# Attention and a token mixer on one core: the first four heads' exponentials and v stay four bytes wide

## The chip, the cores and the metric

One core of one Trainium2 chip runs the whole program. TensorE (PE, with its weight loads PEld), VectorE (DVE), ScalarE (ACT) and GpSimd (POOL) each work through a queue of their own in order; SyncE (SP) issues the transfers. The metric is the device time of one execution in microseconds; three runs of the kernel before stand here.

## The reference, cut to what matters

```python
scores = scale * np.matmul(q, k.transpose(0, 1, 3, 2))      # 8 batches, 8 heads, 576 positions, 64 wide
scores = np.where(block_i >= block_j, scores, -1e9)         # blocks of 64 positions
attn = np.exp(scores - np.max(scores, axis=-1, keepdims=True))
attn = attn / (np.sum(attn, axis=-1, keepdims=True) + 1e-09)
x = np.matmul(attn, v)                                      # heads side by side: 512 channels
theta = x @ w_theta
zr, zi = x * np.cos(theta), x * np.sin(theta)
u = x + w_tok_r @ zr + w_tok_i @ zi                         # over the 576 positions of a batch
out = u + np.maximum(u @ w_ch, 0.0)
```

All inputs and the output are four-byte or wider. The kernel keeps that accuracy mostly by splitting a number into a high and a low two-byte part and making three products: high by high, high by low, low by high.

## The kernel before

A batch is four pairs of heads, 64 heads in all. For a pair, `scores_wide`, `scores_narrow` and `scores_first` make the scores on PE, batches 0 to 2 straight from the four-byte q and k (the constant `WHOLE`), later ones from parts. Per head, DVE takes maxima (`maxima`, L632), ACT the exponentials into the four-byte tile `t` (L645). The exponentials must then be turned, keys to the partitions. For the first eight heads (`PE_TURNED`) PE does it: `turn_up` (L670) transposes blocks of 128 columns into the PSUM banks from which the scores came, `turned_high` copies them as two-byte high parts into the tile `pt` (a copy on ACT or DVE, L430 and L432), `turned_low` subtracts on DVE and writes the low parts (L435). A head has three such pieces at most: A (8 blocks, 1024 columns), B (4 blocks, 512), and for the even head of a pair "4" (1 block). Later heads are split before the turning (`high`, `low`) and turned by transfers. `weighted` (L704) then makes the head's 15 blocks by v, three products a block, with v's high part from `v_first` (L422, L424, L426) and low part from `v_second` (L572, DVE); `normalise` (L716 to L722) divides.

When all heads of a batch are done, the mixer runs: `theta` on PE (L840, L843), the angle's rest and size, sines on ACT (L881, L883), products with x (`times_x`, L892), z's high and low parts (L430, L435), `mix` on PE (L916), u and its parts, `channel` on PE (L939) and the output. The three weight matrices arrive at the start as eight-byte numbers, are cut on ACT, POOL and DVE (L470 to L506), scaled and split.

Nothing is scheduled by itself: `emit` walks the table `ORDER`, a list of step numbers, and so writes each engine's queue; `BANKS` gives each PSUM use its bank and `PLACES` a letter (A, D, P) for each step that may run on more than one engine. The tables cover the whole program, all eight batches.

Of the kernel before, what the change touches and what calls it, by code (L numbers as in the profile page):

```python
# [212 lines left out]
]  # L213
BANKS = (
    "6036634613301236460123451012346501235400123650123100123640123640123540123460123560123560123560123450123540123540"
    "1235401234601235401234601234601234501235401235601235601234601235601236501234601236401236501236524650165044562445"
    "1366654015041066656146605041531566625545056616403655450046560146652046315014405544561042543015410645564641503045"
    "126452542562535304460316014405260435142"
)
# [1011 lines left out]
```

## Time and profile before

| what | us |
|---|---|
| median of 3 runs | 658.3 (657.48 to 658.71) |
| the profiled execution | 657.96 |
| its span, first to last instruction | 656.2 |
| PE busy | 620.3 |
| DVE busy | 578.4 |
| ACT busy | 511.3 |
| POOL busy | 352.3 |

The span is the time between the first and the last instruction; 1.8 us lie around it. Busy time is the time in which at least one instruction of the engine was under way; as matmuls overlap their neighbours, a busy PE need not be at its peak.

### The profile page before, as it was taken

Reading aid. Unit: us, or ns where it says so; the run is one execution under the profiler, and the core shown is the slowest. Engines: PE = TensorE matmul, PEld = TensorE weight load, DVE = VectorE, ACT = ScalarE, POOL = GpSimd, SP = SyncE. Lnnn points to the kernel's source line nnn. Section 1 sums busy time; section 2 is a strip of 40 time slices with the busy share of each in tenths; the row PEclk is TensorE's granted clock in tenths of the full one; section 3 lists DMA queues with packets and bytes.
Section 4 is the critical chain, followed back from the end, with each engine's and each line's share of the span. In section 5 each row is a group of like instructions: output and inputs, shape, how many; then the busy total and the mean of one; then the engine's idle time right before and its main releaser. Section 6 shows DMA issues by size and latency. Waiting matters only on the chain. (4 is left out here: it accounts for less than half of the span.)

```text
span 656.2 us, 18226 instructions
## 1 busy us (share of the span) xinstructions
PE 620.3 (95%) x7474; PEld 459.1 (70%) x7474; DVE 578.4 (88%) x1153; ACT 511.3 (78%) x803; POOL 352.3 (54%) x392
## 2 busy tenths in 40 slices
PE   5689979999999999999999999999999999899997
PEld 3377657775887677767778667875776677757775
DVE  4999999898999898998999999998999988766655
ACT  5999899777975999979988889998998987026212
POOL 4335574553565456545684248654684586553520
PEclk9799996999999999999999999999999999999999
DMA  9965697989698579968997887999898666920101
GB/s 350 394 210 151 110 198 167 209 156 219 141 241 163 116 154 240 204 122 192 214 223 160 147 236 169 181 177 191 178 212 157 114 104 142 179 42 1 56 19 72
DMA packets 242403, 110.03 MB, mean 168 GB/s; under 512 B 229904, under 2 KB 229904, under 8 KB 242320
## 3 DMA queue, kind: packets, MB, share of 16 engines
q1 hardware_dynamic: 242320, 108.88, 76.1%
q8 instruction: 58, 0.95, 0.6%
q14 instruction: 25, 0.20, 0.1%
HBM read 42.01 MB, written 9.44 MB: 78 GB/s over the span
## 5 line engine op out<-in xcount | busy, mean ns | idle before, releaser
L916 PEld LDWEIGHTS <-zh 128*128 128x128 f16 x1152 | 112.7, 98 | 31.5 <-issue 1.7
L916 PE MATMUL g<-wT_h,zh 128*128 128x288 f16 x396 | 113.4, 286 | 2.0 <-DVE xT L955 2.0
L916 PE MATMUL g<-wT_l,zh 128*128 128x288 f16 x396 | 113.2, 286 | 0.0
L916 PE MATMUL g<-wT_h,zl 128*128 128x288 f16 x396 | 113.2, 286 | 0.0
L704 PE MATMUL g<-v,pt 128*128 128x65 f16 x2880 | 100.9, 195 | 7.0 <-DVE xn L722 5.4
L704 PEld LDWEIGHTS <-pt 128*128 128x128 f16 x2880 | 97.4, 98 | 13.3 <-issue 4.5
L632 DVE TENSOR_REDUCE m<-s 128x1 f32<-128x576 f32 (+3 forms) x132 | 85.1, 672 | 2.7 <-PE s L595 2.2
L435 DVE TENSOR_TENSOR p<-t,p 128x1600 f16<-128x1600 f32 (+4 forms) x47 | 78.3, 1668 | 3.1 <-ACT p L430 2.5
L430 ACT CAST p<-t 128x1536 f16<-128x1536 f32 (+4 forms) x51 | 68.0, 1337 | 2.7 <-DMA pt<-p 2.0
L435 POOL TENSOR_TENSOR p<-t,p 128x1536 f16<-128x1536 f32 (+4 forms) x17 | 45.0, 2650 | 46.5 <-ACT p L430 32.0
L916 PEld LDWEIGHTS <-zl 128*128 128x128 f16 x576 | 56.4, 98 | 18.6 <-DVE zl L435 2.1
L645 ACT ACTIVATE t<-s,m,size 128x576 f32<-128x576 f32 (+1 forms) x80 | 59.8, 780 | 7.2 <-POOL m L640 5.2
L840 PEld LDWEIGHTS <-xT 128*128 128x128 f16 x384 | 35.7, 98 | 39.4 <-issue 3.7
L632 DVE TENSOR_REDUCE m<-g 128x1 f32<-128x192 f32 (+2 forms) x156 | 54.1, 370 | 7.6 <-PE g L595 7.5
L939 PEld LDWEIGHTS <-wch_h 128*128 128x128 f16 x512 | 47.8, 98 | 15.8 <-issue 3.3
L435 POOL TENSOR_TENSOR zl<-aa,zh 128x512 f16<-128x512 f32 (+1 forms) x34 | 42.5, 1256 | 27.0 <-ACT zh L430 25.7
L645 ACT ACTIVATE t<-g,m,size 128x320 f32<-128x320 f32 (+2 forms) x100 | 49.4, 535 | 9.7 <-POOL m L640 9.1
L916 PE MATMUL s<-wT_h,zl 128*128 128x288 f16 x180 | 51.5, 286 | 1.8 <-DVE zl L435 1.8
L916 PE MATMUL s<-wT_h,zh 128*128 128x288 f16 x180 | 51.5, 286 | 0.0
L916 PE MATMUL s<-wT_l,zh 128*128 128x288 f16 x180 | 51.5, 286 | 0.0
L892 POOL TENSOR_TENSOR aa<-aa,xn 128x256 f32<-128x256 f32 (+1 forms) x58 | 43.6, 761 | 9.7 <-ACT aa L883 8.5
L939 PE MATMUL g<-uh,wch_h 128*128 128x288 f16 x160 | 45.8, 286 | 1.8 <-ACT t L645 1.2
(199 smaller groups left out, 1668.9 us busy)
## 6 DMA issues: line engine op xcount, KB each, us to landing
rv<-in_v SPq DMA_DIRECT2D x16, 768.0 KB, 5.8
rq<-in_q SPq DMA_DIRECT2D x16, 640.0 KB, 5.6
rk<-in_k SPq DMA_DIRECT2D x16, 576.0 KB, 4.7
out<-xT SPq DMA_DIRECT2D x32, 288.0 KB, 3.6
w_raw<-in_w_tok SPq DMA_DIRECT2D x5, 576.0 KB, 5.8
pt<-in_w_tok SPq DMA_DIRECT2D x4, 576.0 KB, 8.6
w_raw<-in_w_theta SPq DMA_DIRECT2D x4, 512.0 KB, 7.6
w_raw<-in_w_ch SPq DMA_DIRECT2D x4, 512.0 KB, 5.1
```

What stands on the lines that cost most here:

```text
L430: nc.scalar.copy(out=out, in_=x)
L435: engine_of(on).tensor_tensor(out=out, in0=x, in1=y, op=ALU.subtract)
L632: nc.vector.tensor_reduce(out=self.m[:, i:i + 1], in_=self.scores_of(i), axis=AX.X, op=ALU.max)
L645: nc.scalar.activation(out=t_parts[self.hh][:, to:to + n], in_=self.scores_of(i), func=AF.Exp, scale=self.scales()[0], bias=self.m[:, NI + ...
L704: nc.tensor.matmul(o[:, i, :], lhsT=source[:, block, :], rhs=vv[:, slot, hh, :], start=first, stop=last)
L840: nc.tensor.matmul(g, lhsT=xT[:, xx + i, :], rhs=ww[:, dt, :], start=first, stop=last)
L892: engine_of(on).tensor_tensor(out=cd, in0=cd, in1=self.xns[dt][:, i0:i0 + ni, :], op=ALU.mult)
L916: nc.tensor.matmul(g, lhsT=zz[:, kk, cols], rhs=ww[:, kk, ts], start=(n == 0 and kk == k0 and nn == 0), stop=n == 4 and kk == k0 + ni - 1 ...
L939: nc.tensor.matmul(g[:, 0:HS], lhsT=ww[:, dt, e * P:(e + 1) * P], rhs=uu[:, dt, th * HS:(th + 1) * HS], start=dt == 0 and n == 0, stop=dt ...
```

## The change

For heads 0 to 3 the turned exponentials are copied out of PSUM as four-byte numbers, into the room that the two parts had, and v is scaled into a four-byte tile. `turned_low` and `v_second` fall away for them, and `weighted` makes one four-byte product a block. The four-byte v tiles share their room with the q and k parts of batch 3 and later, which become slices of two fixed tiles. `ORDER`, `BANKS` and `PLACES` are new throughout: of the 903 letters 274 differ, of the 375 banks 84; `ORDER` has 3444 steps for 3456.

```diff
+WIDE_HEADS = 4
...
 PLACES = (
-    "ADPPAPPAAPDPPDAPAAPAPDDPPAAPAPPAADAADAPPAAPAAPAAPAAAPADPAPAPAPPAAPAPADAAPAAPAPAPAPPAAPAPAPAADPDPAPPAPPADAPPPPPPP"
...
+    "PDPDAPDDPPDPPDPPAAPAPPAAAAAPAADAPDAAPAPPAAAAAPAAPAADPADPAPAPDPDAAPDPADADPADDAPAPAPPAAPAPAPAAPDDPAPPAPPAPPPAPDAPP"
...
+    room = {"qh": (0, S + D), "kh": (S + D, S), "ql": (2 * S + D, S + D), "kl": (3 * S + 2 * D, S)}
+    qk_room = [const.tile([P, 4 * S + 2 * D], F16, name=f"qk{i}") for i in range(QK_BUFS)]
+    v_wide = [x[:, 0:4 * NV * (D + 1)].bitcast(F32).rearrange("p (a h d) -> p a h d", a=NV, h=2) for x in qk_room]
+    for part in v_wide:
+        nc.gpsimd.memset(part[:, :, :, D:D + 1], 1.0)
+        nc.gpsimd.memset(part[64:P, 0, :, D:D + 1], 0.0)
+        nc.gpsimd.memset(part[0:64, NV - 1, :, D:D + 1], 0.0)
...
         def part(self, tag):
-            return ld.tile([P, S + D if tag[0] == "q" else S], F16, tag=tag, name=tag, bufs=QK_BUFS)
+            at_, n = room[tag]
+            return qk_room[self.p % QK_BUFS][:, at_:at_ + n]
...
         def v_first(self, on):
-            scaled(on, self.v1[:, :, :, 0:D], self.raw("v"), self.mixer.scales["v"].up)
+            to = v_wide[self.p % 2] if 2 * self.p < WIDE_HEADS else self.v1
+            scaled(on, to[:, :, :, 0:D], self.raw("v"), self.mixer.scales["v"].up)
...
+    def wide_of(turned):
+
+        return turned.rearrange("p a c -> p (a c)").bitcast(F32).rearrange("p (a c) -> p a c", c=P)
...
+            if self.n < WIDE_HEADS:
+                at_ = {"A": 4, "B": 0, "4": 12}[piece]
+                return x, wide_of(self.turned)[:, at_:at_ + n, :], None
...
+                if self.n < WIDE_HEADS:
+                    for j, (at_, slot) in enumerate(blocks):
+                        nc.tensor.matmul(o[:, i, :], lhsT=wide_of(source)[:, at_, :], rhs=v_wide[pair.p % 2][:, slot, hh, :],
+                                         start=j == 0, stop=j == len(blocks) - 1)
+                    continue
...
-        add(("v2", p), pair.v_second, [("v1", p)])
+        if 2 * p >= WIDE_HEADS:
+            add(("v2", p), pair.v_second, [("v1", p)])
...
-                        add(("th", n, x), step_of(h.turned_high, x), [("tp", n, x)] + w_free, on="AD")
-                        add(("tl", n, x), step_of(h.turned_low, x), [("th", n, x)],
-                            leaves={"A": [("s1", p, hh, k) for k in range(2)], "B": [("s2", p, hh)], "4": [("t4", n)]}[x])
+                        leaves = {"A": [("s1", p, hh, k) for k in range(2)], "B": [("s2", p, hh)], "4": [("t4", n)]}[x]
+                        add(("th", n, x), step_of(h.turned_high, x), [("tp", n, x)] + w_free, leaves=leaves if n < WIDE_HEADS else (), on="AD")
+                        if n >= WIDE_HEADS:
+                            add(("tl", n, x), step_of(h.turned_low, x), [("th", n, x)], leaves=leaves)
```

## Rows read from the trace of the kernel before

**Rows 1.** The page's head and table of engines: busy us (share), instructions.

```profile
span 656.2 us, 18226 instructions
PE 620.3 (95%) x7474; PEld 459.1 (70%) x7474; DVE 578.4 (88%) x1153; ACT 511.3 (78%) x803; POOL 352.3 (54%) x392
```

**Rows 2.** Stretches: us, busy time (instructions) by engine, PE clock, DMA share, GB/s.

```profile
13.30:23.50 10.20, 5.40 (x43) 4.06 (x43) 10.20 (x17) 10.17 (x18) 4.07 (x6) 1.00 1.02 407
30.30:36.80 6.50, 4.18 (x38) 3.41 (x38) 6.50 (x17) 6.27 (x12) 1.46 (x4) 1.00 0.93 351
36.80:58.10 21.30, 19.39 (x289) 15.56 (x287) 21.24 (x52) 19.10 (x35) 10.70 (x19) 1.00 0.41 133
58.10:73.60 15.50, 15.34 (x252) 11.84 (x251) 15.43 (x42) 14.01 (x27) 9.67 (x13) 1.00 0.79 171
84.00:98.60 14.60, 10.53 (x133) 7.08 (x132) 13.97 (x32) 13.74 (x24) 11.32 (x11) 1.00 1.11 200
98.60:108.80 10.20, 8.78 (x95) 6.79 (x95) 9.47 (x20) 9.75 (x17) 4.26 (x8) 0.50 0.76 171
108.80:142.00 33.20, 33.20 (x426) 26.63 (x425) 29.47 (x73) 26.63 (x44) 18.44 (x16) 1.00 1.06 193
```

**Rows 3.** Timeline of PE: start, length, line, operation, [idle before it <- releaser].

```profile
94.22 0.43 PE L616 MATMUL g<-rk,rq 128*128 128x64 f32 x2
98.93 2.64 PE L704 MATMUL g<-v,pt 128*128 128x65 f16 x45 [4.28 <-DVE xn L722]
...
110.62 0.30 PE L916 MATMUL g<-wT_h,zh 128*128 128x288 f16 x1
```

**Rows 4.** Tile pt, 0 to 120 us: ns min/median/max, first and last start, forms.

```profile
L435 DVE TENSOR_TENSOR pt<-g,pt x10: 252/678/682, 15.0 to 69.1; 128x512 f16<-128x512 f32 x8, 128x128 f16<-128x128 f32 x2
L435 DVE TENSOR_TENSOR pt<-s,pt x10: 251/1214/1225, 21.6 to 65.1; 128x1024 f16<-128x1024 f32 x8, 128x128 f16<-128x128 f32 x2
L430 ACT CAST pt<-g x9: 291/586/611, 14.4 to 67.8; 128x512 f16<-128x512 f32 x8, 128x128 f16<-128x128 f32 x1
```

**Rows 5.** Groups by shape, 0 to 120 us: count | busy us, mean ns | idle before.

```profile
L572 DVE SCALAR_TENSOR_TENSOR v<-rv,size,v 128x768 f16<-128x768 f32 x8 | 8.4, 1048 | 0.0
```

**Rows 6.** Timeline of DVE around two low parts of 1024 columns.

```profile
61.98 2.35 DVE L435 TENSOR_TENSOR pt<-s,pt 128x1024 f16<-128x1024 f32 x2
64.25 0.48 DVE L632 TENSOR_REDUCE m<-g 128x1 f32<-128x320 f32 x1
```

**Rows 7.** Groups by shape, whole span: a four-byte ACT write, v's high part on DVE.

```profile
L470 ACT ACTIVATE w_val<-w_raw 128x512 f32<-128x512 f32 x8 | 5.4, 678 | 6.9 <-DMA w_raw<-in_w_theta 6.7 <-DMA w_raw<-in_w_ch 0.2
...
L424 DVE TENSOR_SCALAR v<-rv,size 128x768 f16<-128x768 f32 x1 | 0.7, 655 | 0.0
```

**Rows 8.** Timeline of PE: one head's products, turnings, a lone four-byte product.

```profile
41.22 1.54 PE L704 MATMUL g<-v,pt 128*128 128x65 f16 x45
42.69 2.17 PE L588 MATMUL s<-rk,rq 64*128 64x512 f32 x16
...
48.11 2.25 PE L670 MATMUL s<-ident_r,t 128*128 128x128 f32 x16 [0.20 <-ACT t L645]
...
83.61 0.33 PE L616 MATMUL g<-rk,rq 128*128 128x64 f32 x2
```

**Rows 9.** Weight loads: timeline of two four-byte products; their group up to 120 us.

```profile
13.64 0.53 PEld L616 LDWEIGHTS g<-rk,rq 128*128 128x128 f32 x4
...
L616 PEld LDWEIGHTS g<-rk,rq 128*128 128x128 f32 x18 | 3.0, 204 | 1.9 <-ACT t L645 1.4
```

**Rows 10.** Timelines of POOL and DVE at 557 us, and line L435 on DVE.

```profile
556.96 3.19 POOL L435 TENSOR_TENSOR p<-t,p 128x1536 f16<-128x1536 f32 x1 [4.97 <-ACT p L430]
...
557.10 3.59 DVE L435 TENSOR_TENSOR zl<-aa,zh 128x512 f16<-128x512 f32 x1
...
L435 DVE TENSOR_TENSOR zl<-aa,zh x14: 410/681/3587, 106.2 to 583.1; 128x512 f16<-128x512 f32 x8, 128x256 f16<-128x256 f32 x6
```

**Rows 11.** One late stretch, columns as in the second group.

```profile
500.00:560.00 60.00, 56.51 (x723) 41.02 (x717) 54.87 (x101) 51.36 (x77) 39.55 (x34) 1.00 0.66 123
```

More of the change, by code (lines that the diff above doesn't have):

```diff
@@ L35 @@
 PE_TURNED = 8
+WIDE_HEADS = 4
 WHOLE = 3
 ORDER = [
[174 rows of a table removed]
[173 rows of a table added]
 ]
 BANKS = (
[L215 to L218, printed above, removed]
+    "6536662522301234630123455012346401235400123650123100123450123640123540123460123560123560123560123450123540123540"
+    "1235401234601235401234601234601234501235401235601235601234601235601236501234601236401236501236534655165044565644"
+    "3131654015640166264154665041566164625545056616413651450146560146651046305104415544654042542015601645564640414045"
+    "123526645163026554423504021346054315062"
@@ L219 @@
 )
 PLACES = (
-    "ADPPAPPAAPDPPDAPAAPAPDDPPAAPAPPAADAADAPPAAPAAPAAPAAAPADPAPAPAPPAAPAPADAAPAAPAPAPAPPAAPAPAPAADPDPAPPAPPADAPPPPPPP"
-    "PDPAPPPADPADPADPAPAPAPDADPADDADAPADPADPPADPDPAPDDPADDPADPPDPAAPADPAPAAAPADPADAAADADPADPPAPADPADAAAPADPADAAAPDDPA"
-    "PAAADADPADPPAPADPADAPAPADPADAAAPADPPDAAPPADPADAPAPADPADAAAPADDAPAAAPADPPPAAPPDDPAPAAADADPADAAAPADPAPAAAPDPPADAAA"
-    "PPPPADPPAPADDAPPPPPAPADAAAAADDPDPPAPDDADDPADDPADDDAPDDAPDDADDDAPDPAPPDDAPAPPAADAAAAAAPAPPPDDDADADPPAPDDAPPDPPDPA"
-    "PDPPPDPADDDADPDPPDDADPPAPPADPPDDPAAAAADAAAPDPDPDDADADAPDAPPPAPPDAPDPAPPPAPPDAPPPADPDAPDPAPPDAPPAPAPPPDADAADDAAPP"
@@ L226 @@
-    "APAPDDDDDADDPAPPPPPPPAPDPPPPDAPPPAPDDAPDPAPDPADPPADDPDAPAPDDAAAAADAAPADPDAPDDDAAPPPPDPPPPDAPDPPPPDADDPAPPPAPPPAP"
-    "DPADPPAPDADPDAPADDDAAADAAPAPAPAPADDDDPPPDPPAPDDAPDPDPPDDDDPAPDPAPPDPDPPAPPPPDDADAPADAAADAADADAPAPAPDDDDADAPPPDDP"
-    "DPPDADPPADPDPPPPPPPDADPPPPPPPDDPADPDPAPAPPDAAAAAAADDPDADADDADDDDPDPDPAPDPAPDDPPPDAPDDAPDDADPPPPDDDDPPAPPADDDADAD"
-    "ADDADAA"
+    "PDPDAPDDPPDPPDPPAAPAPPAAAAAPAADAPDAAPAPPAAAAAPAAPAADPADPAPAPDPDAAPDPADADPADDAPAPAPPAAPAPAPAAPDDPAPPAPPAPPPAPDAPP"
+    "PDPPPPPADPAPPADPADAPADPADPADPAPAPADPPDPPAPPDPAPDDPADAPADPDDAAAPADDAPPPADADDAPPAADADPAPPPAPADDADAPAPADPADAAAPDDPA"
@@ new lines @@
+    "PAAPPADPADPPAPADDADAAAPADPADAAAPADPPDPAAPADDADPAAPADDADAAAPADDPPAAAPADPAPAAPPDDPAPAAAPADDADAAAPADPAPAAAPDPPADPAA"
+    "PAPPAPPPAPADPAPAPPPDPADAAAADPDAPDPAPDPADDPAPPDPDDPPDDDAPDPAPPDAPDPAPDDDPPADAAADAAAAAADAPAPDDADDDAPPAPDPAPPPAPPDP"
+    "PDPADPPADDPADDPPDDDAPPPPDDADAPAPADDAAADADAPADAPADDADDAPPAPPDAPPPAPPPPPPPDPPPAPPPAPPPAPDPADDDAPPAPAPADDDAAADDAAAD"
+    "APPPDDDDDADDDPPPPPDPPAPDDAPPPAPDPAPPPAPPDAPDPAPPDPPPAPPPADAAAAAAADAADADAPAPDADADPPPDPDPPPDPPPPDPPPPDPPAPPPAPPPAP"
+    "PPADPPDPDAPPPADADDAADADAAPAPAPAPADDDDPPPDPPADDPAPPPPDPDAPDDAPDPPPPDADDPAPDPAPPADAPADAAAADAAAAPPADAPDDDDDDADPDPPP"
@@ L230 @@
+    "ADPDAPPDPPDDPPDPADDPPPDDPDDDDDDPAPPPDPDDPAAADAAADDADAPPDADADADADDPPPPAPPDAPDPAPDDPPPDADDDADPDPPPDDPDPAPPADDDPDPA"
+    "AAAADAA"
 )
@@ L1028, in attention_phase_mixer @@
                         for n in ({"q": ["ql"], "k": ["kl"], "v": ["v2"]} if b >= WHOLE else
-                                  {"q": ["s1", "s2", "sd"], "k": ["s1", "s2", "sd"], "v": ["v2"]})[what]]
+                                  {"q": ["s1", "s2", "sd"], "k": ["s1", "s2", "sd"], "v": ["v1" if 2 * p < WIDE_HEADS else "v2"]})[what]]
                 add(("ld", b, what, g), step_of(m.load, what, g), turn_of(f"r{what}{g}", last) + old)
@@ L1051, in keys @@
         return [(name, n, x) for x in pieces(n)]
+    wide_last = {}
     for p in range(B * NPAIR):
@@ L1059, in attention_phase_mixer @@
         s_last = [("s1", p), ("s2", p), ("sd", p)]
+        if 2 * p == WIDE_HEADS - 2 or 2 * p == WIDE_HEADS - 4:
+            used = [x for n in heads for x in keys("weighted", n)]
+            for name in ("qh", "kh", "ql", "kl"):
+                wide_last[name, p % QK_BUFS] = used
         ready = [("ld", b, x, pr // PG) for x in "qk"]
         if b >= WHOLE:
-            add(("qh", p), pair.q_high, [("vc", b, of, 2)] + turn_of("qh", s_last, QK_BUFS), on="PAD")
-            add(("kh", p), pair.k_high, [("vc", b, of, 2)] + turn_of("kh", s_last, QK_BUFS), on="PAD")
-            add(("ql", p), pair.q_low, [("qh", p)] + turn_of("ql", s_last, QK_BUFS))
-            add(("kl", p), pair.k_low, [("kh", p)] + turn_of("kl", s_last, QK_BUFS))
+            add(("qh", p), pair.q_high, [("vc", b, of, 2)] + turn_of("qh", s_last, QK_BUFS) + wide_last.pop(("qh", p % QK_BUFS), []), on="PAD")
+            add(("kh", p), pair.k_high, [("vc", b, of, 2)] + turn_of("kh", s_last, QK_BUFS) + wide_last.pop(("kh", p % QK_BUFS), []), on="PAD")
+            add(("ql", p), pair.q_low, [("qh", p)] + turn_of("ql", s_last, QK_BUFS) + wide_last.pop(("ql", p % QK_BUFS), []))
+            add(("kl", p), pair.k_low, [("kh", p)] + turn_of("kl", s_last, QK_BUFS) + wide_last.pop(("kl", p % QK_BUFS), []))
             ready = [("ql", p), ("kl", p)]
-        add(("v1", p), pair.v_first, [("vc", b, m.scales["v"].of, 2)] + turn_of(f"v{p % 2}", [x for n in heads for x in keys("weighted", n)]),
+        add(("v1", p), pair.v_first, [("vc", b, m.scales["v"].of, 2)] + turn_of(f"v{'w' * (2 * p < WIDE_HEADS)}{p % 2}", [x for n in heads for x in keys("weighted", n)]),
             on="PAD" if b < WHOLE else "APD")
-        add(("v2", p), pair.v_second, [("v1", p)])
+        if 2 * p >= WIDE_HEADS:
+            add(("v2", p), pair.v_second, [("v1", p)])
         wide = [("s1", p, hh, k) for hh in range(2) for k in range(2)]
@@ L1087, in gone, with t_last @@
                 return [(name, n, x) for x in pieces(n) if "all" in (x, piece) or x == piece]
+            def t_last(n):
+                return "th" if n < WIDE_HEADS else "tl"
             def turned_of(n, piece):
                 if n < PE_TURNED:
-                    return [("tl", n, piece)] + [("tl", n, "4") for _ in range(piece == "A" and n % 2 == 0)]
+                    return [(t_last(n), n, piece)] + [(t_last(n), n, "4") for _ in range(piece == "A" and n % 2 == 0)]
                 return [("turn", n, piece)]
@@ L1117, in attention_phase_mixer @@
                     add(("turn", n, piece), step_of(h.turn, piece), [("low", n, piece)] + w_free)
-                needs = turned_of(n, piece) + [("v2", p)] + (turned_of(heads[0], piece) if piece != "B" else []) + o_free
+                needs = turned_of(n, piece) + [("v1" if n < WIDE_HEADS else "v2", p)] + (turned_of(heads[0], piece) if piece != "B" else []) + o_free
                 add(("weighted", n, piece), step_of(h.weighted, piece), needs)
```

347 rows, old and new, of the table ORDER are left out of this document.

## The prediction, made blind

> **What bounds the kernel now.** I read the page's table of engines first [rows 1]: TensorE (PE) is busy 620.3 of 656.2 us, VectorE (DVE) 578.4, so both could be the limit and the average does not say where. The table of stretches decides it [rows 2]. From 13.3 us on DVE is busy in practically all of every stretch up to 98.6 us (10.20 of 10.20, 6.50 of 6.50, 21.24 of 21.30, 15.43 of 15.50, 13.97 of 14.60), while PE has holes: 10.20 - 5.40 = 4.8 us, then 2.3, then 1.9, and 4.1 us between 84.0 and 98.6. From 108.8 on it is the other way round: PE 33.20 of 33.20, DVE 29.47. So there are two kernels: an opening of about 110 us that goes at the pace of DVE (with ScalarE, ACT, not far behind: 19.10 of 21.30, 13.74 of 14.60), and a long rest that goes at the pace of PE. The first matmul of the token mix of batch 0 at 110.62 us [rows 3] marks the border. The four heads of the change have all their work in the opening, so a gain there arrives at the end only as an earlier start of the PE-bound rest, as long as PE has the same work left from that matmul on.
>
> Up to 36.8 us the DMA engines are full as well (share 1.02, then 0.93) [rows 2]; both orders put the same loads and nearly the same DVE work ahead of the last weight of the token matrices, so I count nothing as gained before some 31 us; what is taken off DVE there is filled with work pulled forward, and pays later.
>
> **Part 1, what leaves DVE.** For heads 0 to 3 the low parts go: per head one 1024-column and one 512-column subtraction out of PSUM, for the two even heads one of 128 columns, and for two pairs the low part of v. Durations are 1.214, 0.678 and 0.252 us [rows 4] and 1.048 [rows 5]. But DVE instructions overlap their neighbours a little: two of 1024 columns and the step behind them start at 61.98 and 64.25 [rows 6], so one costs 1.135, about 0.08 less than its duration. With that: 4 x 1.135 + 4 x 0.60 + 2 x 0.17 + 2 x 0.97 = 9.2 us of a full DVE. The first copy of each block stays, now four bytes wide. No four-byte copy out of PSUM is in this trace. ACT's copy to two bytes takes 0.586 for 512 columns [rows 4], its nearest four-byte write 0.678 [rows 7], so the price of the new copies lies between nothing and 0.09 us each (0.6 us on ACT in all); I take nothing, as the source, which is what is read from PSUM, is the same. No DMA is issued by these heads (their blocks are turned on PE), the queues keep their steps, and the new small fills of the ones and zeros beside the four-byte v stand at POOL's start, ahead of any step that DVE waits for. The shared room with the q and k parts is not asked for again before batch 3, when it has long been free.
>
> **Part 2, what the new engine letters move.** I decoded the old and the new tables step by step and compared the sets of steps that stand ahead of that first mix matmul. PE has exactly the same steps there. On DVE 27 steps worth 14.5 us leave (the 9.2 above; five products with x, three z low parts and three weight steps, which go to other engines or behind the matmul, and a few small ones) and 21 come, worth 8.2: two copies of 512 turned columns (0.60 each, the length of the subtraction they resemble), two high parts of v (0.655 less the overlap [rows 7]), weight steps, three maxima of later heads. Net on DVE **-6.3 us**. On ACT 17 steps of 10.4 us leave and 12 of 7.4 come: **-3.0 us**. POOL: 11.9 leave, 11.0 come; it is busy half of the opening and hides that.
>
> **Part 3, what PE gets.** Now a head is 45 two-byte products; they are issued in 42.69 - 41.22 = 1.47 us [rows 8], 0.033 each. After the change it is 15 four-byte products of 65 columns. The trace has no such product, but a close one: the first block's scores, four bytes, 128x128 weights, 64 columns. There a product is two instructions, each with its own weight load: four loads take 0.53 us and one takes 0.204 [rows 9], a pace of (0.53 - 0.20) / 3 = 0.11 us, so 0.22 us a product. Bounds: the four-byte turning of 16 blocks, one instruction each, takes 2.25 us [rows 8], 0.14 each at most; and a lone product of the close kind takes 0.33 us [rows 8]. I take 0.22, the row with the same operands. A head is then 3.3 us, +1.83, and four heads **+7.3 us** of PE, against 4 x (2.10 - 1.47) = +2.5 at the low end (15 x 0.14 a head) and 4 x (4.95 - 1.47) = +13.9 at the high end.
>
> [...]
>
> Where do the 7.3 us go? The four heads' products run between 30.3 and 58.1 us; PE is idle there for 2.3 + 1.9 = 4.2 us [rows 2]. The rest, 7.3 - 4.2 = 3.1 us, makes PE late for the turning and scores that stand behind these products in its queue, and DVE and ACT wait for those.
>
> **The sum.** DVE alone would let the first mix matmul start 6.3 us earlier; less the 3.1 us of waiting for PE that is 3.2; ACT's own work is 3.0 shorter and it has little idle time. I take -3.0. From that matmul on PE has the same work as before, so the end moves by as much: the profiled execution's 657.96 becomes 655.0. That execution was 0.34 us under the median of 658.3; as a median the forecast is **655.3 us**. The clock I leave alone: it fell to half between 98.6 and 108.8 us [rows 2] after PE had nothing from 94.7 to 98.9 [rows 3], the wait for the end of head 8's sums on DVE, and the new order has a like wait there.
>
> **Rivals.** (1) PE takes the wide products without making anyone late, because the search put other work around them, and ACT's idle time gives way: DVE's whole 6.3 us count, 652.0. For it: DVE is the fuller engine in every stretch. Against: ACT at 94% between 84.0 and 98.6. Chance 0.14. (2) A product costs more than 0.22, halfway to the lone one, 0.27: 4 x (4.05 - 1.47) = 10.3 us, 6.1 of them beyond PE's idle time, which eats the 6.3: no change, 658.1. The same comes out if the re-made order loses the gain in the PE-bound rest. Chance 0.20. (3) Slower: the new letters take some 12 us of long subtractions off DVE over the whole run and give them to POOL, four of them whole heads of 3.2 us. At 556.96 us POOL subtracts for 3.19 us, and DVE's z low part, which starts at 557.10, ends only with it: 3.59 us instead of the median 0.681 [rows 10], and in that neighbourhood PE stands still for 60.00 - 56.51 = 3.5 us [rows 11]. Each such meeting on a step that PE waits for costs 3.59 - 0.68 = 2.9 us. Two more of them than before, behind the forecast's gain: 655.3 + 5.8 = 661.1; from the second on the change is slower than before. Against: many such stretched steps cost nothing, as PE has other work queued. Chance 0.24. [...]
>
> **How the numbers follow.** The forecast has 0.42. About 0.2%, 1.3 us, is what a measurement of this kernel can tell from no change. Faster is the forecast and rival 1, 0.56; the same is rival 2, 0.20; slower is rival 3, 0.24. For the range I go to rival 1 below (652.0) and to rival 3's price above (661.0); beyond are half of rival 3, a few hundredths under rival 1, and a product at the lone price (0.33: 13.9 - 4.2 - 6.3 = +3.4, inside). The forecast's own range, with its product between 0.20 and 0.24, is 654 to 656.6.
>
> **What would show it.** Right: in the after profile a wide head's 15 products take 3.2 to 3.4 us as 30 instructions; DVE has idle time between 35 and 58 us, released by PE; the first mix matmul starts near 107.6 us; the stretch behind it is as long as before. Wrong: a head near 2 or near 5 us; the first mix matmul at 110 or later; DVE full from 35 to 58 (then rival 1); or an early first mix and a late end, with more PE idle time after 200 us than before, behind stretched DVE steps (rival 3).

## The result, and the profile after

The changed kernel takes 650.41 us, the median of four runs (648.39 to 652.83), and before 657.96 beside it: a ratio of 0.9886, 95% interval 0.9847 to 0.9924. A second set of runs, further down, gives 0.9889 (0.9863 to 0.9915). So 7.5 us are gained; the forecast was 3.0. The profiled execution took 651.37 us, 6.6 less than before's. One run further down took 672.14 us, 1.5% above the 662.20 of the fastest of its kernel; it counts as slow and is left out of that kernel's median.

The page of after, its head and table of engines, as in [rows 1]:

```profile
span 649.6 us, 18112 instructions
PE 621.8 (96%) x7412; PEld 465.8 (72%) x7414; DVE 568.0 (87%) x1141; ACT 509.4 (78%) x797; POOL 364.4 (56%) x404
```

PE is busy 1.5 us longer than before in a span that is 6.6 us shorter: what went is idle time, 35.9 us of the span before and 27.8 after. The stretches of after, columns as in [rows 2]; the first two are the parts of the span on both sides of the first mix matmul:

```profile
0.00:108.53 108.53, 91.16 (x952) 70.65 (x955) 93.42 (x212) 94.37 (x162) 56.02 (x104) 0.95 0.80 232
108.53:645.50 536.97, 530.65 (x6462) 395.16 (x6461) 473.72 (x929) 414.57 (x635) 308.34 (x300) 1.00 0.75 157
...
13.30:23.50 10.20, 7.26 (x59) 4.89 (x58) 9.33 (x18) 10.13 (x17) 4.06 (x8) 1.00 1.02 416
30.30:36.80 6.50, 5.67 (x53) 4.88 (x53) 6.18 (x14) 6.50 (x12) 4.97 (x6) 1.00 0.83 335
36.80:58.10 21.30, 21.30 (x189) 18.85 (x188) 20.92 (x50) 19.84 (x37) 6.91 (x12) 1.00 0.57 175
84.00:98.60 14.60, 10.20 (x159) 7.43 (x156) 14.08 (x30) 14.46 (x22) 11.57 (x14) 0.97 1.03 207
98.60:108.80 10.20, 10.20 (x82) 7.64 (x83) 6.21 (x14) 8.94 (x17) 6.19 (x7) 0.55 0.78 155
...
500.00:560.00 60.00, 59.16 (x735) 43.31 (x734) 55.02 (x97) 51.52 (x76) 39.22 (x30) 1.00 0.66 125
```

The same two parts of before, same columns:

```profile
0.00:110.62 110.62, 87.54 (x1015) 63.44 (x1015) 99.16 (x220) 96.01 (x166) 55.01 (x100) 0.92 0.81 228
110.62:652.10 541.48, 532.75 (x6464) 395.63 (x6460) 478.60 (x933) 414.84 (x637) 297.25 (x292) 1.00 0.76 155
```

Here the gain splits: the opening is 110.62 - 108.53 = 2.1 us shorter, and the rest, from the first mix matmul to the last product, 541.5 - 537.0 = **4.5 us shorter**. In the stretch from 500 to 560 us PE now stands still for 0.84 us instead of 3.5 [rows 11].

The timeline of PE in after, columns as in [rows 3], shows the wide products of heads 0 and 2 with what follows, the wait at 92.6 us and the first mix matmul:

```profile
27.77 3.46 PE L716 MATMUL g<-qk,pt 128*128 128x65 f32 x30
...
43.33 3.46 PE L716 MATMUL g<-qk,pt 128*128 128x65 f32 x30
46.63 1.04 PE L683 MATMUL s<-ident_r,t 128*128 128x128 f32 x8
...
92.36 0.22 PE L604 MATMUL g<-ones,mask_q 64*128 64x128 bf16 x2
96.13 1.51 PE L725 MATMUL g<-v,pt 128*128 128x65 f16 x45 [3.55 <-POOL rr L913]
...
108.53 0.29 PE L937 MATMUL g<-wT_h,zh 128*128 128x288 f16 x1
```

A wide head is 30 instructions in 46.63 - 43.33 = 3.30 us, as forecast.

**How the profiled runs are compared.** For each kernel of the table I took the opening (up to the first mix matmul) apart into PE's idle time, what PE lost because part of its busy time lay where the granted clock was 0.5 (half of that busy time, an estimate of mine: a wide head took 6.50 us at a clock of 0.50, in the run with wide heads, old tables and the chain moved, and 3.46 at 1.00 in after), and the work that is left; the "rest" is what follows up to PE's last product. Unread products, where a kernel has them, count as work. The kernels themselves are explained under the experiments. For before that is 23.1 idle, 7.4 lost (clock 0.50 from 23.5 to 30.3 and from 98.6 to 108.8) and 80.1 work, together 110.6. These are single executions, and the lost part differs between executions of one kernel.

| kernel | first mix at | idle | lost | work | rest | idle in the rest |
|---|---|---|---|---|---|---|
| before | 110.6 | 23.1 | 7.4 | 80.1 | 541.5 | 8.7 |
| after | 108.5 | 17.4 | 4.7 | 86.5 | 537.0 | 6.3 |
| after, again | 107.8 | 16.3 | 6.1 | 85.4 | 536.2 | 5.7 |
| wide heads, old tables | 116.9 | 21.5 | 8.3 | 87.0 | 539.8 | 8.1 |
| narrow heads, new tables | 118.5 | 27.4 | 12.0 | 79.2 | 536.4 | 5.3 |
| wide, new opening, old rest | 105.1 | 17.2 | 1.7 | 86.2 | 544.9 | 11.1 |
| wide, old opening, new rest | 117.4 | 20.5 | 9.8 | 87.1 | 536.6 | 5.8 |
| low steps gone, old tables | 111.7 | 25.4 | 7.2 | 79.0 | 541.6 | 8.8 |
| wide products alone, old tables | 117.4 | 21.7 | 7.9 | 87.8 | 540.2 | 8.2 |
| wide, old tables, chain moved | 119.8 | 24.9 | 8.0 | 86.9 | 541.8 | 9.5 |
| before, chain moved | 115.5 | 27.2 | 8.6 | 79.6 | 541.4 | 8.7 |
| narrow, old opening, new rest | 114.4 | 25.0 | 10.5 | 78.9 | 536.5 | 5.3 |
| after with 128 unread products | 105.5 | 14.2 | 0.0 | 91.3 | 536.8 | 6.1 |
| before with 144 unread products | 110.4 | 21.7 | 4.6 | 84.1 | 539.0 | 7.1 |
| narrow, old opening, new rest, 144 unread | 111.7 | 21.0 | 6.2 | 84.6 | 538.1 | 6.7 |

The kernels with the new tables behind the first mix have a rest of 536 to 537 us, whatever their opening, and 538.1 in the one with 144 unread products; the kernels with the old ones 539 to 542 (the mixed one of 544.9 pays 3 us of idle time and 1.7 of clock at its seam, between 105 and 125 us). Among the old ones, a rest of 541.4 to 541.8 goes with the meeting of VectorE and GpSimd of [rows 10], behind which PE waits 1.77 us, and one of 539.0 to 540.2 with profiled executions that do not have that wait; set against the latter, the new tables save 2 to 4 us, and what is more is that one meeting.

### The profile page after: what moved, and what is told of

Read it like the earlier page. It is cut to its first block, busy times and chain, and to the rows that moved or that the text cites. A ratio compares the mean times of both kernels' runs of the same rounds, so it can differ in the third digit from the quotient of the medians.

```text
span 649.6 us, 18112 instructions
## 1 busy us (share of the span) xinstructions
PE 621.8 (96%) x7412; PEld 465.8 (72%) x7414; DVE 568.0 (87%) x1141; ACT 509.4 (78%) x797; POOL 364.4 (56%) x404
## 4 chain that ended last, share of the span: by engine, by line
PE 65%; ACT 13%; DMA 7%; DVE 7%; issue 4%; POOL 4%; SPq 0%; DVEq 0%; ACTq 0%; POOLq 0%
PE g L937 15%; PE s L937 9%; PE g L725 7%; PE g L861 6%; PE g L960 6%; PE s L597 5%; PE s L861 5%; ACT t L658 3%; PE s L960 3%; DMA pt<-in_w_tok 3%; PE g L597 2%; DMA pt<-p 2%; PE g L716 2%; ACT aa L904 1%; PE s L864 1%
## 5 line engine op out<-in xcount | busy, mean ns | idle before, releaser
L937 PE MATMUL g<-wT_h,zh 128*128 128x288 f16 x369 | 105.6, 286 | 0.6 <-DVE xT L976 0.5
L937 PE MATMUL g<-wT_l,zh 128*128 128x288 f16 x369 | 105.5, 286 | 0.0
L937 PE MATMUL g<-wT_h,zl 128*128 128x288 f16 x369 | 105.5, 286 | 0.0
L645 DVE TENSOR_REDUCE m<-s 128x1 f32<-128x448 f32 (+3 forms) x132 | 85.2, 674 | 6.6 <-PE s L604 6.4
L442 POOL TENSOR_TENSOR p<-t,p 128x1536 f16<-128x1536 f32 (+4 forms) x22 | 59.6, 2710 | 52.9 <-ACT p L437 33.7
L442 DVE TENSOR_TENSOR p<-t,p 128x1600 f16<-128x1600 f32 (+4 forms) x42 | 70.5, 1683 | 4.0 <-ACT p L437 2.5
L437 ACT CAST p<-t 128x1600 f16<-128x1600 f32 (+4 forms) x52 | 69.0, 1332 | 0.6
L960 PEld LDWEIGHTS <-wch_h 128*128 128x128 f16 x512 | 48.1, 98 | 14.2 <-issue 2.1
L645 DVE TENSOR_REDUCE m<-g 128x1 f32<-128x320 f32 (+2 forms) x156 | 54.1, 373 | 2.9 <-PE g L604 2.8
L913 POOL TENSOR_TENSOR rr<-rr,xn 128x256 f32<-128x256 f32 x38 | 36.6, 971 | 32.7 <-ACT rr L902 32.2
L658 ACT ACTIVATE t<-g,m,size 128x192 f32<-128x192 f32 (+2 forms) x100 | 49.6, 535 | 6.1 <-POOL m L653 5.2
```

The lines of the kernel that those rows point to most:

```text
L437: nc.scalar.copy(out=out, in_=x)
L442: engine_of(on).tensor_tensor(out=out, in0=x, in1=y, op=ALU.subtract)
L645: nc.vector.tensor_reduce(out=self.m[:, i:i + 1], in_=self.scores_of(i), axis=AX.X, op=ALU.max)
L658: nc.scalar.activation(out=t_parts[self.hh][:, to:to + n], in_=self.scores_of(i), func=AF.Exp, scale=self.scales()[0], bias=self.m[:, NI + ...
L913: engine_of(on).tensor_tensor(out=cd, in0=cd, in1=self.xns[dt][:, i0:i0 + ni, :], op=ALU.mult)
L937: nc.tensor.matmul(g, lhsT=zz[:, kk, cols], rhs=ww[:, kk, ts], start=(n == 0 and kk == k0 and nn == 0), stop=n == 4 and kk == k0 + ni - 1 ...
```

## The experiments

Theories at the outset: the gain is made in the opening, by what VectorE is spared (the prediction's own reason); or behind it, by the new tables; or by the granted clock.

### The tables and the wide heads, each without the other

**Wide heads on the old tables.** The code of after, the order, banks and letters of before without the steps that are gone (shown against after).

```diff
 PLACES = (
-    "PDPDAPDDPPDPPDPPAAPAPPAAAAAPAADAPDAAPAPPAAAAAPAAPAADPADPAPAPDPDAAPDPADADPADDAPAPAPPAAPAPAPAAPDDPAPPAPPAPPPAPDAPP"
+    "ADPPAPPAAPDPPDAPAAPAPDDPPAAPAPPAADAADAPPAAPAAPAAPAAAPADPAPAPAPPAAPAPADAAPAAPAPAPAPPAAPAPAPAADPDPAPPAPPADAPPPPPPP"
...
```

> The changed program's code (four wide heads) with the order, banks and engine letters of before; the steps that are gone are struck out of the order, nothing else moves. Opening theory (what the wide heads take off VectorE ahead of the first mix carries the gain): the first mix comes 2 to 3 us earlier than before's 110.6 and the time is near 655. Rest theory (most of the gain is the new tables behind the first mix, where the 543 to 561 us stall is gone): the stall is still there and the time is 655 to 658, so this run alone leaves 5 to 7 us of the 7.5 missing. Clock theory (the gain is the half-clock stretch at 23.5 to 30.3 us that is gone): that stretch decides, and the time is near 651 where it is gone.

Measured: 664.09 us, ratio 1.0094 (1.0074 to 1.0115). **Slower** than before by 6.2 us; none of the theories had that. PE's timeline and the stretch in which the wide heads now lie:

```profile
36.71 3.56 PE L726 MATMUL g<-qk,pt 128*128 128x65 f32 x30
43.04 3.46 PE L726 MATMUL g<-qk,pt 128*128 128x65 f32 x30
...
36.80:58.10 21.30, 20.60 (x174) 17.78 (x174) 12.63 (x32) 14.60 (x27) 5.81 (x10) 1.00 0.27 97
```

VectorE is relieved, 12.63 of 21.30 where before had 21.24 [rows 2], but PE is nearly full there, 20.60, and the border comes at 116.9 us. In after the first wide head starts at 27.77 instead of 36.71.

**Narrow heads on the new tables.** The low steps stand right behind their high steps; pairs 0 and 1 have their own room for two-byte parts of v.

```diff
-WIDE_HEADS = 4
+WIDE_HEADS = 0
...
-            self.v1, self.v2 = v_parts[p % 2]
+            self.v1, self.v2 = (early if p < 2 else v_parts)[p % 2]
```

> The new tables with the first four heads as in before: their low parts, the second part of v and the three two-byte products a block are back, each low step right behind its high step; pairs 0 and 1 keep their own room for v, so the order is kept whole. VectorE gets the 9.2 us of before back in the opening. Opening theory: the first mix comes 5 to 9 us later than after's 108.5 and the whole gain is lost or more, 657 to 660. Rest theory: the opening loses some 2 to 5 us, the 4 to 5 us gained behind the first mix stay, and the time is 652 to 655.

Measured: 662.36 us, 1.006 (1.0039 to 1.008). The opening is 118.5 us, against 108.5 in after and 110.6 in before; the rest is 536.4. So the opening's tables pay only with wide heads, while the rest keeps its gain.

**New opening with old rest, and the reverse.** In the first the letters change behind the first mix, in the second ahead of it (shown against after):

```diff
-    "PPADPPDPDAPPPADADDAADADAAPAPAPAPADDDDPPPDPPADDPAPPPPDPDAPDDAPDPPPPDADDPAPDPAPPADAPADAAAADAAAAPPADAPDDDDDDADPDPPP"
+    "DPADPPAPDADPDAPADDDAAADAAPAPAPAPADDDDPPPDPPAPDDAPDPDPPDDDDPAPDPAPPDPDPPAPPPPDDADAPADAAADAADADAPAPAPDDDDADAPPPDDP"
```

```diff
-    "PDPDAPDDPPDPPDPPAAPAPPAAAAAPAADAPDAAPAPPAAAAAPAAPAADPADPAPAPDPDAAPDPADADPADDAPAPAPPAAPAPAPAAPDDPAPPAPPAPPPAPDAPP"
+    "ADPPAPPAAPDPPDAPAAPAPDDPPAAPAPPAADAADAPPAAPAAPAAPAAAPADPAPAPAPPAAPAPADAAPAAPAPAPAPPAAPAPAPAADPDPAPPAPPADAPPPPPPP"
```

> After's order, banks and letters up to the first mix product; every step that is left then comes in the order, with the banks and letters, of before. Opening theory: the first mix at 108.5 us and the time as after, 650 to 651. Rest theory: the first mix at 108.5, but the stall at 543 to 561 us is back and the time is 655 to 656.5.

> Before's order, banks and letters up to the first mix product (with the wide heads' lost steps struck out), then every step that is left in the order, with the banks and letters, of after. Opening theory: as the old tables with wide heads, near 655 or above. Rest theory: no stall at 543 to 561 us, the first mix one or two us later than after's 108.5, and 651 to 653.

Measured: 657.37 us, 1.0005 (0.9979 to 1.0031), and 659.22 us, 1.0014 (0.9999 to 1.0028). With wide heads the new rest is worth 1.0094 - 1.0014 = 0.8% behind the old opening and 1.0005 - 0.9886 = 1.2% behind the new one: 5 to 8 us. The larger figure is no clean one: the mixed kernel pays 4.7 us at its seam, and four of its twelve runs took 661 to 663 us. PE's timeline of the first of the two still shows a wait that before has too and after has not:

```profile
546.45 0.28 PE L970 MATMUL g<-uh,wch_h 128*128 128x288 f16 x1 [1.21 <-ACT t L668]
```

**The new rest alone, behind before's own opening with narrow heads.**

```diff
 ORDER = [
-    160, 158, 8, 0, 16, 9, 32, 40, 24, 10, 11, 334, 333, 1, 56, 339, 2, 338, 362, 363, 350, 17, 351, 3, 370, 18, 352,
+    160, 158, 8, 0, 16, 32, 24, 40, 335, 9, 10, 1, 334, 367, 11, 366, 375, 2, 17, 3, 56, 12, 339, 18, 376, 48, 340,
...
-WIDE_HEADS = 4
```

> Before's code, narrow heads and opening; from the first mix product on, every step that is left in the order, with the banks and engine letters, of after (a step that is in neither order of after stands right behind its high step). If the new tables behind the first mix are a gain of their own, as the wide heads on old opening with new rest against the wide heads on old tables have it (659.2 against 664.1), 653 to 655 and no idle time of TensorE over 0.3 us between 540 and 600 us. If they only fit the new opening, 657 to 660.

Measured: 653.51 us, 0.9907 (0.9876 to 0.9938), 6 us, though its profiled opening was 3.8 us longer than before's (10.5 us lost to the clock instead of 7.4). The clock is not where the 6 us come from: its granted mean was 0.982 to 0.990 in these runs and 0.981 to 0.989 in those of before beside them. The part of its span behind the first mix, columns PE busy, PEclk, DMA share, GB/s:

```profile
114.40:650.90 536.50, 531.21 (x6464) 1.00 0.74 158
```

**That settles the largest part: the new tables behind the first mix gain without any wide head.** After is 0.9886 and 0.9889; what the wide heads and the new opening add to 0.9907 is 0.2%, some 1.3 us and no more than the intervals.

**Order or letters.** After's order and banks with the letters of before on the 274 steps whose letter the change turned.

```diff
 PLACES = (
-    "PDPDAPDDPPDPPDPPAAPAPPAAAAAPAADAPDAAPAPPAAAAAPAAPAADPADPAPAPDPDAAPDPADADPADDAPAPAPPAAPAPAPAAPDDPAPPAPPAPPPAPDAPP"
+    "ADPPAPPAAPDPPDAPAAPAPDDPPAAPAPPAADAADAPPAAPAAPAAPAAAPADPAPAPAPPAAPAPADAAPAAPAPAPAPPAAPAPAPAADPDPAPPAPPADAPPPPPPP"
...
```

> After with its own order and banks, but with the engine letters of before for all 274 steps whose letter the change turned. If the order carries the gain of the new tables, 650 to 653. If the letters carry it (which engine does which step), 656 to 664. Behind 540 us: if the stall-free end belongs to the order, TensorE idles there for less than 0.5 us as in after; if to the letters, 2 us or more come back.

Measured: 700.62 us, 1.0625 (1.0586 to 1.0663), far beyond both; PE is idle for 33.0 us between 125 and 540 us, where after has 6.2. Order and letters are one thing; the question which of the two carries the gain has no answer.

### What the two halves of the code change cost on the old tables

**The low steps struck out, the two-byte products kept.**

```diff
-                    for nn, (block, vv) in enumerate(((high, pair.v1), (high, pair.v2), (low, pair.v1))):
+                    for nn, (block, vv) in enumerate(((high, pair.v1),) * 3 if self.n < 4 else ((high, pair.v1), (high, pair.v2), (low, pair.v1))):
...
-        add(("v2", p), pair.v_second, [("v1", p)])
+        if p > 1:
+            add(("v2", p), pair.v_second, [("v1", p)])
```

> Before's code and tables with part 1 of the change alone: the low steps of the first four heads and the second part of v of pairs 0 and 1 are struck out, and nothing else moves. TensorE keeps its three two-byte products a block (each of the three reads the high part and the first part of v, so the low terms of these heads are left out of the result). If VectorE bounds the opening step for step, as the prediction's first term has it, the first mix comes 6 to 9 us earlier than before's 110.6 and the time is 649 to 652. If the opening hangs on TensorE's order, the clock or the loads instead, the first mix moves by less than 3 us and the time is 655 to 658.

Measured: 658.03 us, 0.999 (0.9974 to 1.0005). **The 9.2 us that leave VectorE are worth nothing by themselves, in the old order.** Timelines of VectorE, of GpSimd and of PE in this run:

```profile
21.66 0.44 DVE L509 TENSOR_SCALAR wT_h<-w_val 128x576 uint16<-128x576 uint16 x1
24.41 0.15 DVE L759 TENSOR_REDUCE size<-size 128x1 f32<-128x2 f32 x1 [2.30 <-ACT junk L811]
...
29.23 0.65 POOL L487 TENSOR_SCALAR w_raw<-w_raw 128x512 int32<-128x512 uint8 x1 [4.19 <-DMA w_raw<-in_w_ch]
29.98 0.37 POOL L376 TENSOR_SCALAR diag<-ident_r,size 128x128 bf16<-128x128 f32 x1
...
30.40 0.27 PE L382 MATMUL g<-diag,ones 128*128 128x128 bf16 x1 [4.65 <-POOL diag L376]
```

VectorE now stands still for 2.30 us ahead of a small reduction that needs ScalarE's sums of v, and GpSimd brings the diagonal that comes of it only behind a weight step that waited 4.19 us for its load. PE waits 4.65 us for that diagonal and multiplies it at 30.40 us; in before it did so at 30.86, so that product comes only 0.46 us earlier.

**The wide products, the low steps kept as dead work.**

```diff
         def turned_low(self, piece):
             x, hi, lo = self.turned_parts(piece)
+            if self.n < WIDE_HEADS:
+                lo, hi = (y[:, 0:x.shape[1] * P].rearrange("p (a c) -> p a c", c=P) for y in (dead, none))
             less("D", lo, x, hi)
```

> Part 3 of the change alone, on before's tables: the four-byte products of the first four heads, while VectorE still does all 12 low steps at their old places, into room that nobody reads. Prediction's third term: 3.1 us come through to the first mix, 661. If TensorE has no cover for the wide products in the old order, the full 7.3 us come through, 665. If the two parts only add up, this run and the one with the low steps struck out differ from before by amounts whose sum is the 5.9 us of the wide heads on old tables.

Measured: 665.05 us, 1.0111 (1.008 to 1.0141), 7.3 us by the ratio and 6.7 by the medians: the price of the products comes through, in full as far as the interval tells. With the experiment above, the two halves add up: -0.1% and +1.1% against +0.9% for both.

**Three copies handed from ScalarE to VectorE**, once with the low steps gone, once with wide heads:

```diff
-    "ADPPAPPAAPDPPDAPAAPAPDDPPAAPAPPAADAADAPPAAPAAPAAPAAAPADPAPAPAPPAAPAPADAAPAAPAPAPAPPAAPAPAPAADPDPAPPAPPADAPPPPPPP"
+    "ADPPAPPAAPDPPDAPAAPAPDDPPAAPAPPAADAADAPPAAPAAPAAPAAAPDDPDPDPAPPAAPAPADAAPAAPAPAPAPPAAPAPAPAADPDPAPPAPPADAPPPPPPP"
```

> The run with the low steps struck out, and in addition three high copies of heads 0 and 1 handed from ScalarE to VectorE at their places in the old order (2.4 us of ScalarE's time between 19 and 22 us, where VectorE then stood idle until 24.4 us behind the reduction that waits for ScalarE's sums of v). The low terms of these heads are left out of the result, as there. ScalarE theory (in the old order ScalarE is as full as VectorE, so what VectorE gives up turns into a wait for ScalarE): the reduction starts near 22.0 instead of 24.4 us, and the first mix comes 1.5 to 2.5 us earlier than without the hand-over; 655.5 to 656.5. Order theory (TensorE's fixed order holds the opening, whoever computes the steps before): no change, 658.

> The four wide heads on before's tables, and the same three copies handed from ScalarE to VectorE. ScalarE theory: 1.5 to 2.5 us off the 664.1 of the wide heads on old tables, 661.5 to 662.5. Order theory: no change, 664; then the wide products must stand elsewhere in TensorE's order to pay, as they do in after (the first at 27.8 us instead of 36.7).

Measured: 658.41 us, 0.9999 (0.9985 to 1.0014), and 664.92 us, 1.0108 (1.0069 to 1.0148). No gain: ScalarE alone was not what held the opening. PE's timeline of the first says what came instead: the next scores waited for a bank that VectorE emptied:

```profile
22.90 4.11 PE L597 MATMUL s<-rk,rq 64*128 64x512 f32 x16 [2.48 <-DVE pt L441]
```

**One chain moved ahead in the old order**, with wide heads (shown against wide heads on the old tables) and without:

```diff
 ORDER = [
...
-    51, 368, 345, 96, 104, 80, 346, 165, 88, 347, 163, 161, 387, 60, 20, 398, 381, 348, 65, 36, 73, 166, 28, 66,
-    97, 410, 399, 411, 98, 52, 418, 99, 105, 44, 5, 409, 400, 13, 408, 112, 106, 21, 159, 167, 81, 384, 412, 82,
-    29, 413, 136, 414, 385, 168, 137, 169, 401, 89, 389, 83, 415, 390, 107, 391, 170, 67, 402, 120, 171, 113,
+    51, 368, 345, 96, 104, 80, 346, 165, 88, 347, 163, 161, 387, 60, 20, 398, 399, 400, 381, 348, 5, 13, 21, 65,
+    36, 73, 166, 167, 28, 29, 66, 97, 410, 411, 136, 168, 98, 169, 170, 171, 172, 52, 418, 99, 105, 44, 409,
+    408, 112, 106, 159, 81, 384, 412, 82, 413, 414, 332, 385, 137, 401, 89, 389, 83, 415, 349, 355, 390, 107,
...
```

166 to 172 are the steps of v's scale (167 the diagonal on GpSimd, 168 the product), 5, 13, 21, 29 and 136 theta's size, 399 and 400 head 2's first exponentials, 332 the four-byte v of pair 0, 349 and 355 head 0's weighted products.

> The four wide heads on before's tables, letters and banks as they were, with one chain moved ahead in the old order: GpSimd's diagonal of v's scale ahead of the two weight steps that wait for loads, theta's four size products and their reduction, the product on that diagonal, v's scale steps, head 2's first two exponentials ahead of four weight steps on ScalarE, and head 0's wide products ahead of the transposes of head 2. Queue theory (the old order holds this chain behind weight loads that come when they come): v's scale is known near 28 us instead of 33.3, head 0's wide products start near 31 instead of 36.7 us, and 2 to 5 us come off the 664.1 of the wide heads on old tables: 659 to 662. Rival (TensorE's own 7.3 us of wide work is the whole loss, wherever it stands): 663 to 665.

> Before with the same chain moved ahead and narrow heads. Queue theory with VectorE as the next bound (it has 9.2 us more to do here): 0 to 2 us off before's 658.3. If the chain alone holds the opening, whatever VectorE does, 2 to 5 us off, 653 to 656, and then the reorder and not the wide heads is the gain.

Measured: 667.93 us, 1.012 (1.0088 to 1.0153), and 662.82 us, 1.0043 (1.0022 to 1.0063). The second is slower than before; the first is no faster than without the move (1.0094, 1.0074 to 1.0115). The queue theory falls in this form. PE's timeline of the first:

```profile
26.08 0.23 PE L390 MATMUL g<-diag,ones 128*128 128x128 bf16 x1 [0.79 <-DVE size_theta L534]
31.47 1.97 PE L693 MATMUL s<-ident_r,t 128*128 128x128 f32 x8 [4.72 <-ACT t L668]
33.23 6.50 PE L726 MATMUL g<-qk,pt 128*128 128x65 f32 x30
```

The product on the diagonal came at 26.08 as meant, but behind it PE waited 4.72 us for exponentials of head 3 that ScalarE brought no earlier (31.4 us, against 31.0 without the move), the granted clock was 0.50 from 27.9 to 41.5 us, and the wide head took 6.50 us in it instead of 3.46. What this move freed, the next queue took back. Which set of moves the search found to break that is not isolated.

### The granted clock

**Unread products ahead of the half-clock stretch, in after.** First 96 into the bank of the weighted sums, then 96 and 128 into a bank that is free:

```diff
         def weighted(self, piece):
             pair, hh = self.pair, self.hh
+            if (self.n, piece) == (10, "B"):
+                for _ in range(128):
+                    nc.tensor.matmul(banks[6][:, 0:56], lhsT=ones, rhs=ones[:, 0:56], start=True, stop=True)
```

> After with 96 products of 56 columns that nobody reads, placed on TensorE ahead of head 10's weighted products, in the 3.55 us of idle time before 96.1 us that stand ahead of the half-clock stretch at 97.6 to 107.8. Clock theory: the clock stays full there, the 4.7 us that the stretch costs TensorE come back, and the time is 645 to 648. Rival: the granted clock halves all the same, or VectorE and ScalarE end last behind 97 us, and the time stays at 650 to 651. If the filler overruns its gap it costs up to 1 us.

> After itself once more, beside the other runs of this call: 650 to 651, the half-clock stretch at 97.6 to 107.8, no idle time of TensorE over 0.3 us between 540 and 600 us. If its gain behind 540 us was a matter of one profiled execution, an idle time of 1 to 2 us shows up there.

> After with 96 products of 56 columns that nobody reads ahead of head 10's weighted products, this time into bank 6, which is free from 84.9 us on, so that they run in the 3.55 us of idle time and not behind it (in the earlier run they waited for the same normalisation as the products they were to bridge to, and took 4.64 us behind the gap). Clock theory: no half-clock stretch at 97.6 to 107.8, 646 to 648. Rival: the clock halves there all the same, or VectorE and ScalarE end last, 650 to 651.

> After with 128 unread products in its 3.55 us of idle time ahead of 96.1 us, so that 0.6 us of it or less stay idle (96 left 1.5 us). Clock theory: no half-clock stretch behind 95 us in any run, so that what is left of it is the earlier ones: 0.984 to 0.987 of before. Rival: as after and as with 96 of them, 0.988 to 0.989.

Measured: the first 652.78 us, 0.9896 (0.9861 to 0.9932), misplaced: its products waited 3.46 us for the normalisation, like the ones behind them. After beside it 650.89, 0.9889 (0.9863 to 0.9915), with 0.1 us of idle time of PE behind 540 us, as in the first profile. With 96 in the free bank 651.83, 0.9877 (0.9849 to 0.9905): two of its six runs had a mean granted clock of 1.000 and took 647.4 and 648.8 us, four had 0.988 or 0.989 and took 651.8 to 652.8. With 128: **647.87 us, 0.983 (0.9812 to 0.9847)**, clocks 0.998 to 1.000 in all runs. It beats both kernels. PE's timeline and the stretches of its profiled run, columns of the latter as in [rows 2]:

```profile
93.29 3.48 PE L712 MATMUL g<-ones 128*128 128x56 bf16 x128
97.41 1.53 PE L728 MATMUL g<-v,pt 128*128 128x65 f16 x45 [0.65 <-DMA pt<-p]
...
84.00:98.60 14.60, 13.96 (x284) 10.84 (x282) 13.85 (x29) 14.27 (x21) 11.72 (x12) 1.00 1.04 211
98.60:108.80 10.20, 9.83 (x117) 7.20 (x114) 9.69 (x24) 10.17 (x21) 8.19 (x12) 1.00 1.01 190
```

Where after had a clock of 0.55 from 98.6 to 108.8 us, it is 1.00 in both stretches, and the first mix comes at 105.5.

**The same in before, and in before with the new rest.** 144 products ahead of its 98.9 us.

```diff
+            if (self.n, piece) == (10, "A"):
+                for _ in range(144):
+                    nc.tensor.matmul(banks[5][:, 0:56], lhsT=ones, rhs=ones[:, 0:56], start=True, stop=True)
```

> Before with 144 products of 56 columns that nobody reads in its 4.28 us of idle time ahead of 98.9 us, into bank 5, which is free from 89.7 us on. Clock theory: the half-clock stretch at 98.6 to 108.8 (8.78 us busy in it, so 4.4 us lost) shrinks or goes, and the time is 654 to 657. Rival: VectorE and ScalarE end last there, 658.

> Before with narrow heads and its own opening, the new tables behind the first mix, and the 144 unread products in the idle time ahead of 98.9 us. If the two single gains (6.3 and 5.1 us on that chip) add, 0.983 of before, 647 to 649, and no wide head is needed for it. If the filler only gives back what a later stage then waits for, 0.990, as the new tables alone.

Measured: 654.71 us, 0.9923 (0.9897 to 0.9948), and 651.91 us, 0.9901 (0.9881 to 0.9921). In before the filled gap is worth 5 us; the stretch at half clock behind 98.6 is gone from its profile. Where in the program the 5 us are made the profiled execution does not show: it has two earlier stretches at 0.50, 22.7 to 29.6 and 36.4 to 39.8 us, its first mix comes at 110.4, and of the 2.5 us by which its rest is shorter than before's, 1.8 are the wait at the meeting of [rows 10], which it does not have. PE's timeline around the filled gap:

```profile
97.86 3.88 PE L696 MATMUL g<-ones 128*128 128x56 bf16 x144
102.01 1.52 PE L707 MATMUL g<-v,pt 128*128 128x65 f16 x45 [0.26 <-DVE xn L725]
105.36 2.17 PE L588 MATMUL s<-rk,rq 64*128 64x512 f32 x16 [1.84 <-ACT t L645]
```

With the new rest the filler adds nothing that the intervals show (0.9901 after 0.9907). Its profile has two early stretches at 0.50, 23.1 to 29.9 and 33.3 to 40.1 us, and behind the border PE waits 1.3 us up to 130 us, where the run without filler has no wait before 130. After with 128 unread products is faster than this kernel, 0.983 against 0.9901, 4.7 us by the ratios. That is not the wide heads and the new opening alone: in the profiles the opening of after with the filler has 6.8 us less idle time and 6.7 us more work, and the 6.2 us that the other lost to the early stretches. After's own profiles have no early stretch in the first and one, 27.1 to 30.5, in the second; whether the new opening keeps the early clock up by itself is not settled.

## Why the prediction was wrong, step by step

- **The border and the two limits**: right as a description. Behind the first mix PE is busy 530.65 of 536.97 us.
- **Part 3, PE's price**: right. 30 instructions in 3.30 us, two a product; PE's work in the opening grows by 6.4 us in after and 6.9 on the old tables, where 7.3 was forecast.
- **Where PE's price goes**: mis-sized, and on the wrong grounds. The forecast hid 4.2 us in PE's idle time. On the old tables idle time falls by only 1.6 us (23.1 to 21.5) and the whole price arrives; in after by 5.7: there the first wide head starts at 27.77 us and PE is busy for all of the stretch from 36.8 to 58.1.
- **Parts 1 and 2, the opening goes at VectorE's pace**: the count was about right, the reason failed. VectorE's busy time ahead of the first mix falls by 5.7 us (99.16 to 93.42), where 6.3 was forecast, and the four-byte copies cost nothing extra (in after ScalarE's of 1024 columns take 1.028 us in the mean with four bytes and 1.027 with two). But full rows of VectorE [rows 2] said that it had no idle time, not that its work was what others waited for; ScalarE's row in the same stretch, 10.17 of 10.20, was as full, and the loads' share was 1.02. Without the low steps the first mix did not come earlier (111.7 against 110.6), and idle time appeared on VectorE. In after VectorE is still full from 36.8 to 58.1 us, 20.92 of 21.30, which the prediction had named as a sign against itself.
- **The sum at the border, -3.0**: near, -2.1 and in the repeat -2.8, but by luck. The -2.1 are 6.4 us more of PE's work, 5.7 less of its idle time and 2.7 less lost to the clock, not VectorE's 6.3 less 3.1 of waiting, and only the tables and the wide heads together have it: either alone loses 6 to 8 us at the border.
- **The clock left alone**: a term was missing. After's two profiles lost 4.7 and 6.1 us where before's lost 7.4. The half-clock stretch behind 98 us did come back, as said, and the filled gap shows that it was worth removing.
- **"From that matmul on PE has the same work as before, so the end moves by as much"**: this is the step that failed. The matmuls are the same (6462 and 6464 records), but the tables behind the border were new too, and I valued them at nothing, or, in the second and third rival, at a loss. They gain 4.5 us in the profile and 6 us in the run that has them alone, and the prediction's own sign, "the stretch behind it is as long as before", did not come. The 4.5 us are 2.4 of idle time of PE (8.7 to 6.3) and 2.1 of busy time (532.75 to 530.65). The idle time is saved at the end alone: behind 545 us before's PE is idle for 3.3 us, behind 540 after's for 0.1; ahead of that it is 5.4 and 6.2. Two waits of before's PE are gone, timeline columns as above:

```profile
547.42 0.28 PE L939 MATMUL g<-uh,wch_h 128*128 128x288 f16 x1 [1.20 <-ACT t L645]
...
560.75 0.30 PE L916 MATMUL s<-wT_h,zl 128*128 128x288 f16 x1 [1.77 <-DVE zl L435]
```

The second belongs to the meeting of [rows 10], which the third rival had. The new tables no longer have the meeting, but that wait is also missing from half of the profiles with the old ones (see the last section), while the first wait is in all ten of them. The same operation of VectorE in after, ns min/median/max:

```profile
L442 DVE TENSOR_TENSOR zl<-aa,zh x14: 412/682/971, 110.2 to 619.2; 128x512 f16<-128x512 f32 x10, 128x256 f16<-128x256 f32 x4
```

Why the same matmuls are busy for 2.1 us less is not settled.

The profile of before had shown that gain as possible: 8.7 us of idle time of PE behind the border, 3.5 of it in one stretch [rows 11]. The diff said that the whole of the tables had been searched anew; a forecast has to give such a search a chance of collecting what idle time there is, not of spoiling it alone.

## What to carry to other kernels

When a change re-makes the schedule of the whole program, price the schedule by the idle time that the bounding engine has in each part, also where the code change does not reach. A full row of an engine is no proof that it is the bound: before work is taken off it, look whether another engine's row in the same stretch is as full, and who waits for whom. And where the granted clock is half behind an idle gap of TensorE, a few unread products in a free bank, no longer than the gap, are worth trying: here they brought after from 650.9 to 647.9 us. With the new rest behind before's opening they brought nothing that the intervals show, so the gain has to be measured.
